# Sums of two query blocks under one guard and one reciprocal, and small VectorE operations made by GpSimd, in attention followed by a Fourier-mixing feed-forward layer

## The chip, the cores and the metric

The kernel runs on one core of one Trainium2 chip. The metric is the device time of one execution in microseconds, the median of several. The core has five engines that run side by side, each through its own list of instructions in order, and wait for one another by semaphores: PE (TensorE, matrix products), DVE (VectorE), ACT (ScalarE), POOL (GpSimd) and SP (SyncE, which here issues transfers).

## The reference

Sliding-window attention with four sink tokens (4 batches, 8 heads, 768 tokens, 64 per head, window 128), then a two-dimensional Fourier transform of the result, a layer norm and a feed-forward layer:

```python
scores = np.where(is_sink | in_window, scale * q @ k.T, -1e9)
scores = scores - np.max(scores, axis=-1, keepdims=True)
a = np.exp(scores)
a = a / (np.sum(a, axis=-1, keepdims=True) + 1e-09)
x = a @ v                                    # heads side by side: 768 x 512
u = x + np.real(np.fft.fft(np.fft.fft(x, axis=1), axis=2))
un = (u - mean(u)) / np.sqrt(var(u) + 1e-6)
out = u + np.maximum(un @ w_ch1, 0.0) @ w_ch2
```

## The kernel before

**Attention.** A batch is six blocks of 128 queries, `g` counts the 24 blocks of all batches. A block is worked in four steps, one for a pair of heads (`hp`). In each, PE makes the scores in PSUM (L701, L703), DVE merges the two key blocks (`merge`, L709) and takes mask and minimum (`soft1`, L721), ACT takes the exponential and its sum (`expo`, L727), POOL splits the sink columns (`sink_p`, L738, L739), PE transposes (L755), ACT copies (L762), POOL cuts the window by two affine_selects (`newer_p` L771, `older_p` L779), and PE multiplies with the values (`av`, L793). The tile `mx` of a block (128 x 3 x 8) holds the minima of its 8 heads in row 0, the sums in row 1, and in row 2 the guarded sums and their reciprocals: POOL adds 1e-9 (`floor`, L747), DVE inverts (`inverse`, L743), and when the block's output is in PSUM, DVE multiplies it by row 2 into `u` (`store_x`, L821).

**Order.** The program walks through 96 steps and 14 more. `STEP_LAG` and `BLOCK_AT` say how many steps behind the scores an operation stands (`floor` 6, `inverse` 8, `store_x` 13 after the first step of its block), and `SCHEDULE` the order on each engine within a step. Work of other stages hangs on steps as events, `at(step, engine, function)`, and runs at the entry "V" (DVE), "A" (ACT), "G" (POOL) or "T" (PE) of the step's list. Up to step 97 the order is as written; behind it the framework's scheduler places the instructions, and it may draw some of them forward between the written ones.

**Fourier.** When the fourth block of a batch is stored, `fourier` hangs up that batch's transform: folds of `u` (L352, L359, L362), split into a high and a low part (L365, L368), two stages of products (L395, L422, L443) and updates of `u` (L459, L460), half of the folds and, but in the last batch, most updates on POOL. The first token of a batch is worked apart. Its row `xr` is loaded in 33 copies; `put_row` (L381) copies it into `u`, `mid_sum` (L372) adds its reversed half, and `mid_row` (L376, L378) puts it, high and low, into `sph`, which the last product of the first stage reads (L395, `za<-cst_row,sph`). These four instructions hang on "V" 5, 8 and 10 steps after the folds' start.

**First group's normalisation.** `normalize` takes the statistics of the first four blocks of the first batch; `deviations` computes 1/sqrt(var) for them by a guess (L522, L524) and four Newton steps of three instructions on 128x4 (L527, L529, L531), hung on "V" of steps 72 to 80. At step 81 `un_make` (L539) normalises the first block on DVE.

**Feed-forward.** Weights are read as integers, put together on DVE (L591 to L593), split on ACT (L608) and POOL (L609); PE makes the two products (L620, L1126) for seven groups of blocks, with ACT and DVE between them (L1114, L1119). The other groups' `deviations` run on DVE. (`general` marks a second program for other parameters, which these inputs do not take.)

Of the kernel before, what the change touches and what calls it, by code (L numbers as in the profile page):

```python
# [11 lines left out]
F32 = mybir.dt.float32  # L12
# [7 lines left out]
P = 128  # L20
# [186 lines left out]
def kernel(  # L207
# [63 lines left out]
    def run(general):  # L271
        tag = "g" if general else ""
        with ExitStack() as p1:
# [59 lines left out]
            def fourier(b, at, ready):  # L333
# [35 lines left out]

                def mid_sum():  # L370
                    r = t_["x0"]
                    V.tensor_tensor(r[:, 1:256], r[:, 1:256], r[:, 511:256:-1], op=ALU.add)  # L372

                def mid_row():
                    t = t_["x0"]
                    V.tensor_copy(sph[:NR, :257], t[:, :257])  # L376
                    lo = sph[NR - 1:NR, :257]
                    V.tensor_tensor(lo, t[NR - 1:NR, :257], f32(lo), op=ALU.subtract)  # L378

                def put_row():  # L380
                    V.tensor_copy(u[NHALF][0:1], t_["x0"][0:1])  # L381
# [94 lines left out]
                at(ready[0] + ROW[0], "V", put_row)  # L476
                at(ready[0] + ROW[1], "V", mid_sum)
                at(ready[0] + ROW[2], "V", mid_row)
# [39 lines left out]
            def deviations(b, blk, n):  # L518
# [6 lines left out]
                for _ in range(4):  # L525
                    yield
                    V.scalar_tensor_tensor(t, y, -0.5, x, op0=ALU.mult, op1=ALU.mult)  # L527
                    yield
                    V.tensor_tensor(t, t, y, op=ALU.mult)  # L529
                    yield  # L530
                    V.scalar_tensor_tensor(y, t, 1.5, y, op0=ALU.add, op1=ALU.mult)  # L531
# [27 lines left out]
            def normalize(s0, s1, s2, get_bank):  # L559
# [6 lines left out]
                steps = deviations(0, 0, n)  # L566
                for i in range(14):
                    at(s1 + i * (s2 - s1) // 14, "V", lambda: next(steps, None))
# [67 lines left out]
            def window_attention(fourier, load_constants):  # L636
                with ExitStack() as pa:
# [73 lines left out]
                    def soft1(g, hp):  # L711
# [4 lines left out]
                        if hp == 0:  # L716
                            st["mx", g] = aw.tile([P, 3, H], F32, tag="mx", name=f"mx_{g}", bufs=4)
                        sm, mx = st["sm", g, hp // 2], st["mx", g]
# [5 lines left out]
                    def expo(g, hp):  # L724
                        sm, mx = st["sm", g, hp // 2], st["mx", g]
# [15 lines left out]
                    def inverse(g):  # L741
                        mx = st["mx", g]
                        V.reciprocal(mx[:, 2], mx[:, 2])  # L743

                    def floor(g):
                        mx = st["mx", g]
# [72 lines left out]
                    def store_x(g):  # L819
                        u = uview(g // NB)  # L820
                        V.tensor_tensor(u[Q_BLOCKS[g % NB]].rearrange("p (h d) -> p h d", h=H), st.pop(("x", g)),  # L821
                                        st.pop(("mx", g))[:, 2, :, None].broadcast_to([P, H, D]), op=ALU.mult)
# [516 lines left out]
```

## Time and profile before

| | before |
|---|---|
| median of 3 runs | 784.29 us (782.91 to 787.69) |
| profiled execution | 786.08 us |
| its span, first to last instruction | 784.1 us |
| busy: PE | 755.7 us (96%) |
| busy: DVE | 453.5 us (58%) |
| busy: ACT | 237.1 us (30%) |
| busy: POOL | 185.1 us (24%) |
| mean granted TensorE clock | 0.991 |

The profile is one execution. An engine is busy while one of its compute instructions runs; waiting, branching and issuing transfers do not count. Matmuls are pipelined and their ends are modelled, so a busy PE is not a PE at its peak. Attention and most of the Fourier work lie in the first 215 us, with the feed-forward layer from there to the end; the two overlap between about 180 and 300 us. Times within the span are counted from its first instruction. "<-" in a row of waits names what ended the wait.

### The profile page before, as it was taken

What the parts mean: (1) busy time and instruction counts of PE and PEld (TensorE: products, weight loads), DVE (VectorE), ACT (ScalarE), POOL (GpSimd) and SP (SyncE); (2) the same over time, 40 slices, a digit from 0 to 9 for tenths busy, and PEclk for the clock granted to TensorE, in tenths of its full rate; (3) what the DMA queues carried; (4) which work ended last, traced back from release to release, by engine and by line L of the source; (5) the groups of instructions that cost most, each with busy time, mean ns of one, the idle gap of its engine ahead of it and who ended that gap; (6) DMA issues with size and microseconds to landing.
All of it is one profiled execution on the core that took longest, in us unless ns stands there. A gap on an engine that the chain in (4) does not pass through costs nothing.

```text
span 784.1 us, 11917 instructions
## 1 busy us (share of the span) xinstructions
PE 755.7 (96%) x4379; PEld 616.8 (79%) x4379; DVE 453.5 (58%) x1330; ACT 237.1 (30%) x704; POOL 185.1 (24%) x307
## 2 busy tenths in 40 slices
PE   7999998989998999999999999999999999999996
PEld 5676876867777878899888888888888888888895
DVE  6878587999999489561456424661456424611211
ACT  4887765766523123221111101111111111110110
POOL 2567477477654255100000000000000000000000
PEclk9999999999999899999999999999999999999998
DMA  9863535434215266110100002000200001000100
GB/s 283 268 177 105 151 83 177 127 112 145 86 50 166 92 196 208 66 59 1 54 0 1 1 18 89 1 0 1 81 0 1 2 1 54 1 0 1 54 1 31
DMA packets 41810, 57.67 MB, mean 74 GB/s; under 512 B 2796, under 2 KB 27500, under 8 KB 41360
## 3 DMA queue, kind: packets, MB, share of 16 engines
q1 hardware_dynamic: 41456, 53.07, 21.6%
q0 software_dynamic: 288, 3.76, 1.3%
q8 instruction: 36, 0.59, 0.3%
q14 instruction: 30, 0.25, 0.1%
HBM read 47.37 MB, written 9.45 MB: 72 GB/s over the span
## 4 chain that ended last, share of the span: by engine, by line
PE 80%; DVE 9%; POOL 4%; issue 3%; ACT 2%; DMA 2%; SPq 1%; POOLq 0%; DVEq 0%; ACTq 0%
PE o L1126 33%; PE h L620 33%; PE s L703 3%; PE xt L793 3%; PE pt L755 2%; PE za L395 1%; DVE cv L592 1%; DVE cv L593 1%; DVE sm L721 1%; PE zb L395 1%; ACT pta L762 1%; ACT sm L727 1%; DMA vt<-in_v_sink_dram 1%; POOL ptl L771 1%; DVE s L709 1%
## 5 line engine op out<-in xcount | busy, mean ns | idle before, releaser
L1126 PE MATMUL o<-w,h 128*128 128x512 f32 x876 | 218.6, 397 | 0.0
L1119 DVE SCALAR_TENSOR_TENSOR h<-h,h 128x512 fp32r<-128x512 f32 (+1 forms) x107 | 65.4, 611 | 250.5 <-ACT h L1114 250.3
L1126 PEld LDWEIGHTS o<-w,h 128*128 128x128 f32 x876 | 164.5, 190 | 36.0
L1114 ACT ACTIVATE h<-h 128x512 fp32r<-128x512 f32 (+1 forms) x107 | 57.1, 534 | 368.6 <-PE h L620 362.4
L620 PE MATMUL h<-un_slots,w 128*128 128x512 f32 (+1 forms) x576 | 124.7, 365 | 0.0
L620 PEld LDWEIGHTS h<-un_slots,w 128*128 128x128 f32 x576 | 99.6, 188 | 19.6
L620 PE MATMUL h<-un_last,w 128*128 128x512 f32 (+1 forms) x432 | 89.0, 355 | 0.0
L620 PEld LDWEIGHTS h<-un_last,w 128*128 128x128 f32 x432 | 72.7, 188 | 12.8
L727 ACT ACTIVATE sm<-sm,mx 128x132 f32<-128x132 f32 x192 | 76.0, 400 | 6.0 <-DVE mx L721 6.0
L1150 DVE STREAM_TRANSPOSE unf<-un 32x128 f32<-32x128 f32 x224 | 67.7, 302 | 3.2
L703 PE MATMUL s<-ring,q 64*128 64x260 f32 x320 | 49.9, 418 | 8.9 <-DVE mx L721 5.3
L721 DVE CUSTOM_DVE_ANT_0 sm<-s,mask 128x132 f32<-128x132 f32 x192 | 48.5, 293 | 6.3 <-PE s L701 1.3
L703 PEld LDWEIGHTS s<-ring,q 64*128 64x128 f32 x320 | 27.3, 188 | 21.6 <-issue 8.0
L609 POOL TENSOR_TENSOR w<-cv,w 128x512 fp32r<-128x512 f32 x25 | 34.1, 1366 | 30.5 <-ACT w L608 30.5
L793 PE MATMUL xt<-ptl,ldv 128*64 128x128 f32 x384 | 39.3, 285 | 0.2 <-POOL ptl L771 0.2
L727 ACT ACTIVATION_READ_ACCUMULATOR sm<-sm,mx 128x1 f32 x192 | 36.7, 191 | 0.0
L1126 PE MATMUL o<-w_ring,h 128*128 128x512 f32 x144 | 35.6, 393 | 0.0
L762 ACT COPY pta<-pt 128x512 f32<-128x512 f32 x48 | 28.0, 583 | 24.9 <-PE pt L755 23.5
L709 DVE COPY_PREDICATED s<-older,s 128x256 f32<-128x256 uint8 x80 | 33.7, 421 | 1.6 <-PE s L703 1.6
L771 POOL TENSOR_SCALAR_AFFINE_SELECT ptl<-pta 128x512 f32<-128x512 f32 x48 | 32.5, 678 | 7.3 <-ACT pta L762 7.2
L793 PEld LDWEIGHTS xt<-ptl,ldv 128*64 128x64 f32 x384 | 21.9, 136 | 15.1 <-issue 6.2
L793 PE MATMUL xt<-pta,ldv 128*64 128x128 f32 x320 | 31.7, 274 | 0.3 <-POOL pta L779 0.3
(197 smaller groups left out, 1039.4 us busy)
## 6 DMA issues: line engine op xcount, KB each, us to landing
raw<-in_moe_w_ch_dram SPq DMA_DIRECT2D x32, 512.0 KB, 3.7
ldv<-in_v_dram SPq DMA_DIRECT2D x28, 256.0 KB, 3.3
ring<-in_qk_dram SPq DMA_DIRECT2D x24, 264.0 KB, 4.8
out_dram<-u SPq DMA_DIRECT2D x24, 256.0 KB, 2.1
q<-in_qk_dram SPq DMA_DIRECT2D x20, 256.0 KB, 4.4
cst<-in_dft_dram POOLq DMA_DIRECT2D x1, 3348.0 KB, 12.8
ud<-us SPq DMA_DIRECT2D x12, 256.0 KB, 2.1
u<-ud SPq DMA_DIRECT2D x2, 1024.0 KB, 4.9
```

The lines of the kernel that those rows point to most:

```text
L620: T.matmul(ps[:, :tb], a[:, cs], x[:, :, cc, :], start=n == 0, stop=n == 3 * NCC - 1)
L703: T.matmul(ps[:, j, :P + W], st["q", g][rows, hp, :], keys(g, 2 * hp + j), start=True, stop=True)
L709: V.copy_predicated(ps[:, :, P + NS:P + W], older[qi > 2], ps[:, :, 0:P])
L721: V.tensor_tensor_reduce(sm[:, h % 4], ps[:, j, P:P + W], mask[min(qi, 3)], -SCALE, 3.0e38, ALU.add, ALU.min, accum_out=mx[:, 0, h:h + 1])
L727: A.activation(sm[:, h % 4], sm[:, h % 4], AF.Exp, bias=mx[:, 0, h:h + 1], scale=-1.0, accum_out=mx[:, 1, h:h + 1])
L762: A.copy(a, st.pop(("pt", g, hp // 2)))
L771: G.affine_select(lo, a, [[0, 4], [s, P]], compare_op=ALU.is_ge, fill=0.0, base=0, channel_multiplier=-s)
L793: T.matmul(ps[D * j:D * j + D, p, :], st["v", kb(g) - i][:, h, :], a[:, h % 4, :], start=i == 0, stop=i == n - 1)
L1114: A.activation(h[0], ps[:, :tb], AF.Relu)
L1119: V.scalar_tensor_tensor(h[1], ps[:, :tb], 0.0, f32(h[0]), op0=ALU.max, op1=ALU.subtract)
L1126: T.matmul(po[i], a[:, ts_], x, start=f == 0 and n == 0, stop=f == NF - 1 and n == 2)
L1150: V.transpose(unf[32 * q:32 * q + 32, :, r], un[r].rearrange("p (c q j) -> p c q j", c=NCC, q=4)[:, :, q])
```

## The change

Three edits.

1. Two blocks share a tile `mx` of 128 x 3 x 2 x 8 (three buffers for four). `floor` and `inverse` do nothing for a block of even `g`, and for one of odd `g` handle both blocks, 16 columns.
2. `put_row`, `mid_sum` and `mid_row` are made by POOL, at the entry "G" of the same steps.
3. Of the first group's Newton steps all but the guess are made by POOL. A scalar_tensor_tensor becomes, in the first place, a product (the factor -0.5 goes to the third), in the third a tensor_scalar and a product: four instructions for three.

```diff
+                R = V if general else G
+
                 def mid_sum():
                     r = t_["x0"]
-                    V.tensor_tensor(r[:, 1:256], r[:, 1:256], r[:, 511:256:-1], op=ALU.add)
+                    R.tensor_tensor(r[:, 1:256], r[:, 1:256], r[:, 511:256:-1], op=ALU.add)
 
                 def mid_row():
                     t = t_["x0"]
-                    V.tensor_copy(sph[:NR, :257], t[:, :257])
+                    R.tensor_copy(sph[:NR, :257], t[:, :257])
                     lo = sph[NR - 1:NR, :257]
-                    V.tensor_tensor(lo, t[NR - 1:NR, :257], f32(lo), op=ALU.subtract)
+                    R.tensor_tensor(lo, t[NR - 1:NR, :257], f32(lo), op=ALU.subtract)
 
                 def put_row():
-                    V.tensor_copy(u[NHALF][0:1], t_["x0"][0:1])
+                    R.tensor_copy(u[NHALF][0:1], t_["x0"][0:1])
...
-                at(ready[0] + ROW[0], "V", put_row)
-                at(ready[0] + ROW[1], "V", mid_sum)
-                at(ready[0] + ROW[2], "V", mid_row)
+                at(ready[0] + ROW[0], "V" if general else "G", put_row)
+                at(ready[0] + ROW[1], "V" if general else "G", mid_sum)
+                at(ready[0] + ROW[2], "V" if general else "G", mid_row)
...
-            def deviations(b, blk, n):
+            def deviations(b, blk, n, eng=V):
...
                     yield
-                    V.scalar_tensor_tensor(t, y, -0.5, x, op0=ALU.mult, op1=ALU.mult)
+                    if eng is V:
+                        V.scalar_tensor_tensor(t, y, -0.5, x, op0=ALU.mult, op1=ALU.mult)
+                    else:
+                        G.tensor_tensor(t, y, x, op=ALU.mult)
                     yield
-                    V.tensor_tensor(t, t, y, op=ALU.mult)
+                    eng.tensor_tensor(t, t, y, op=ALU.mult)
                     yield
-                    V.scalar_tensor_tensor(y, t, 1.5, y, op0=ALU.add, op1=ALU.mult)
+                    if eng is V:
+                        V.scalar_tensor_tensor(y, t, 1.5, y, op0=ALU.add, op1=ALU.mult)
+                    else:
+                        G.tensor_scalar(t, t, -0.5, 1.5, op0=ALU.mult, op1=ALU.add)
+                        G.tensor_tensor(y, t, y, op=ALU.mult)
...
-                steps = deviations(0, 0, n)
+                steps = deviations(0, 0, n, V if general else G)
                 for i in range(14):
-                    at(s1 + i * (s2 - s1) // 14, "V", lambda: next(steps, None))
+                    at(s1 + i * (s2 - s1) // 14, "V" if i < 2 or general else "G", lambda: next(steps, None))
...
-                        if hp == 0:
-                            st["mx", g] = aw.tile([P, 3, H], F32, tag="mx", name=f"mx_{g}", bufs=4)
-                        sm, mx = st["sm", g, hp // 2], st["mx", g]
+                        if hp == 0 and g % 2 == 0:
+
+                            st["mx", g // 2] = aw.tile([P, 3, 2, H], F32, tag="mx", name=f"mx_{g}", bufs=3)
+                        sm, mx = st["sm", g, hp // 2], st["mx", g // 2][:, :, g % 2]
...
                     def inverse(g):
-                        mx = st["mx", g]
+                        if g % 2 == 0:
+                            return
+                        mx = st["mx", g // 2]
                         V.reciprocal(mx[:, 2], mx[:, 2])
 
                     def floor(g):
-                        mx = st["mx", g]
+                        if g % 2 == 0:
+                            return
+                        mx = st["mx", g // 2]
                         G.tensor_scalar_add(mx[:, 2], mx[:, 1], 1e-9)
```

What it moves, at the three places of which the prediction speaks (line numbers of the changed kernel are a few higher). First POOL at steps 76 to 78, before; `sk` are the sink columns, `ptl` and `pta` the cut probabilities, `f` a fold, `mx` the guard:

```order
L738 CAST sk_2272<-sm_0_2167 128x2x16
L739 TENSOR_TENSOR sk_2272<-sm_0_2167,sk_2272 128x2x16
L771 AFFINE_SELECT ptl_3_2300<-pta_3_2266 128x512
L352 TENSOR_TENSOR f_2_0_2302<-u_65 128x512
L779 AFFINE_SELECT pta_3_2266<-pta_3_2266 128x512
L738 CAST sk_2272<-sm_2_2240 128x2x16
L739 TENSOR_TENSOR sk_2272<-sm_2_2240,sk_2272 128x2x16
L771 AFFINE_SELECT ptl_1_2366<-pta_1_2330 128x512
L747 TENSOR_SCALAR mx_2168<-mx_2168 128x8
L359 TENSOR_TENSOR f_2_0_2293<-f_2_0_2302 128x255
```

And now; `stat` are the Newton steps, two or four rows of them in nearly every step:

```order
L748 CAST sk_2244<-sm_0_2140 128x2x16
L749 TENSOR_TENSOR sk_2244<-sm_0_2140,sk_2244 128x2x16
L532 TENSOR_TENSOR stat_0_1875<-stat_0_1875 128x4
L534 TENSOR_TENSOR stat_0_1875<-stat_0_1875 128x4
L785 AFFINE_SELECT ptl_3_2272<-pta_3_2240 128x512
L539 TENSOR_SCALAR stat_0_1875<-stat_0_1875 128x4
L540 TENSOR_TENSOR stat_0_1875<-stat_0_1875 128x4
L352 TENSOR_TENSOR f_2_0_2276<-u_65 128x512
L793 AFFINE_SELECT pta_3_2240<-pta_3_2240 128x512
L532 TENSOR_TENSOR stat_0_1875<-stat_0_1875 128x4
L534 TENSOR_TENSOR stat_0_1875<-stat_0_1875 128x4
L748 CAST sk_2244<-sm_2_2212 128x2x16
```

Between the rows of the attention there are now Newton rows, sixteen in all over nine steps; the guard of the even block is gone. The last two Newton rows stand right ahead of the next fold of this kind (`f_2_1`), a dozen rows behind this piece.

The second place is POOL in the second batch, now; `u` are updates of the first batch:

```order
L761 TENSOR_SCALAR mx_1377<-mx_1377 128x16
L359 TENSOR_TENSOR f_1_1_1645<-f_1_1_1654 128x255
L748 CAST sk_1750<-sm_0_1648 128x2x16
L749 TENSOR_TENSOR sk_1750<-sm_0_1648,sk_1750 128x2x16
L461 TENSOR_TENSOR u_64<-u_64,d_1_1641 128x257
L462 TENSOR_TENSOR u_64<-u_64,d_1_1641 128x255
L378 CAST sph<-xr_1431 33x257
L380 TENSOR_TENSOR sph<-xr_1431,sph 1x257
L785 AFFINE_SELECT ptl_3_1776<-pta_3_1744 128x512
```

The two `sph` rows stand between an update and the affine_select, where before the one followed the other; they were on DVE.

The third is POOL at the end of the attention, where the scheduler decides, before and then now:

```order
L609 TENSOR_TENSOR w_ring<-cv_3180,w_ring 128x512
L771 AFFINE_SELECT ptl_3_3074<-pta_3_3053 128x512
L779 AFFINE_SELECT pta_3_3053<-pta_3_3053 128x512
L460 TENSOR_TENSOR u_65<-u_65,d_2_3141 128x255
L459 TENSOR_TENSOR u_65<-u_65,d_2_3141 128x257
```

```order
L618 TENSOR_TENSOR w_ring<-cv_3148,w_ring 128x512
L785 AFFINE_SELECT ptl_3_3042<-pta_3_3021 128x512
L793 AFFINE_SELECT pta_3_3021<-pta_3_3021 128x512
L383 COPY us_3_2593<-xr_2996 1x512
L374 TENSOR_TENSOR xr_2996<-xr_2996 33x255
L378 CAST sph<-xr_2996 33x257
L380 TENSOR_TENSOR sph<-xr_2996,sph 1x257
L462 TENSOR_TENSOR u_65<-u_65,d_2_3109 128x255
```

All four row operations of the last batch stand in one run between the last affine_select and the first update, and are gone from DVE's list. In all, DVE has 40 instructions fewer (12 reciprocals, 12 Newton, 16 for the rows), POOL 20 more (16 Newton and 16 for the rows, less 12 guards).

## Rows read from the trace of the kernel before

**Rows 1.** The page, part 1: busy microseconds, share of the span, instructions.
```profile
PE 755.7 (96%) x4379; PEld 616.8 (79%) x4379; DVE 453.5 (58%) x1330; ACT 237.1 (30%) x704; POOL 185.1 (24%) x307
```

**Rows 2.** Busy time by stretch: length, engines' busy us, granted clock, DMA share, GB/s.
```profile
15.00:100.00 85.00, 82.36 (x747) 61.27 (x748) 64.46 (x303) 63.18 (x246) 49.42 (x109) 0.98 0.59 181
145.40:185.00 39.60, 35.77 (x319) 28.26 (x316) 38.37 (x144) 25.98 (x98) 29.58 (x50) 1.00 0.35 108
185.00:205.00 20.00, 18.42 (x163) 14.74 (x162) 17.54 (x56) 14.04 (x49) 14.29 (x26) 1.00 0.36 117
205.00:255.00 50.00, 45.75 (x266) 39.19 (x264) 49.32 (x78) 16.58 (x34) 27.46 (x22) 0.99 0.33 106
400.00:784.00 384.00, 377.38 (x1727) 310.66 (x1726) 156.44 (x407) 50.54 (x90) 0.00 (x0) 0.99 0.05 17
```

**Rows 3.** Waits of POOL, 145.4 to 185: us in total, times, longest.
```profile
POOL sk L738 <- ACT sm L727: 6.2, 5, 2.4
```

**Rows 4.** Groups on DVE, 145.4 to 185: count | busy us, mean ns | idle before.
```profile
L531 DVE SCALAR_TENSOR_TENSOR stat<-stat 128x4 f32<-128x4 f32 x4 | 2.5, 613 | 0.0
...
L529 DVE TENSOR_TENSOR stat<-stat 128x4 f32<-128x4 f32 x4 | 2.2, 546 | 0.1
...
L527 DVE SCALAR_TENSOR_TENSOR stat<-stat 128x4 f32<-128x4 f32 x4 | 1.1, 276 | 0.0
...
L743 DVE RECIPROCAL mx<-mx 128x8 f32<-128x8 f32 x4 | 0.8, 198 | 0.0
```

**Rows 5.** Groups over the whole span: operations on the first token's row.
```profile
L378 DVE TENSOR_TENSOR sph<-xr,sph 1x257 fp32r<-1x257 f32 x4 | 2.0, 498 | 0.1
...
L372 DVE TENSOR_TENSOR xr<-xr 33x255 f32<-33x255 f32 x4 | 1.6, 410 | 0.0
...
L376 DVE CAST sph<-xr 33x257 fp32r<-33x257 f32 x4 | 1.6, 398 | 0.0
...
L381 DVE COPY us<-xr 1x512 f32<-1x512 f32 x2 | 0.8, 406 | 0.0
```

**Rows 6.** Time line of DVE: start, us, line, operation, shapes.
```profile
152.43 0.19 DVE L743 RECIPROCAL mx<-mx 128x8 f32<-128x8 f32 x1
152.54 1.21 DVE L531 SCALAR_TENSOR_TENSOR stat<-stat 128x4 f32<-128x4 f32 x1
153.67 0.68 DVE L352 TENSOR_TENSOR f<-u 128x512 f32<-128x512 f32 x1
...
166.35 0.64 DVE L539 TENSOR_SCALAR un<-u,stat 128x512 f32<-128x512 f32 x1
```

**Rows 7.** Time line of POOL, the same stretch.
```profile
152.45 1.27 POOL L352 TENSOR_TENSOR f<-u 128x512 f32<-128x512 f32 x1
...
160.47 1.27 POOL L352 TENSOR_TENSOR f<-u 128x512 f32<-128x512 f32 x1
```

**Rows 8.** Groups on POOL, 145.4 to 185.
```profile
L460 POOL TENSOR_TENSOR us<-us,d 128x255 f32<-128x255 f32 x5 | 4.3, 866 | 0.0
...
L359 POOL TENSOR_TENSOR f<-f 128x255 f32<-128x255 f32 x3 | 2.3, 764 | 0.5 <-DVE f L362 0.3
...
L739 POOL TENSOR_TENSOR sk<-sm,sk 128x32 fp32r<-128x32 f32 x8 | 2.1, 268 | 0.7
...
L738 POOL CAST sk<-sm 128x32 fp32r<-128x32 f32 x8 | 1.9, 236 | 6.2 <-ACT sm L727 6.2
...
L747 POOL TENSOR_SCALAR mx<-mx 128x8 f32<-128x8 f32 x4 | 1.5, 387 | 0.3
```

**Rows 9.** Chain of work, 98 to 128: start, us, engine, tile, line.
```profile
116.65 1.05 POOL u L460
...
123.89 0.24 POOL mx L747
```

**Rows 10.** Time line of POOL: the end of the attention.
```profile
210.91 0.97 POOL L779 TENSOR_SCALAR_AFFINE_SELECT pta<-pta 128x512 f32<-128x512 f32 x1
216.31 1.85 POOL L460 TENSOR_TENSOR u<-u,d 128x255 f32<-128x255 f32 x1 [4.43 <-DVE d L448]
```

More of the change, by code (lines that the diff above doesn't have):

```diff
@@ L724, in expo @@
                     def expo(g, hp):
-                        sm, mx = st["sm", g, hp // 2], st["mx", g]
+                        sm, mx = st["sm", g, hp // 2], st["mx", g // 2][:, :, g % 2]
                         for h in range(2 * hp, 2 * hp + 2):
@@ L821, in store_x @@
                         V.tensor_tensor(u[Q_BLOCKS[g % NB]].rearrange("p (h d) -> p h d", h=H), st.pop(("x", g)),
-                                        st.pop(("mx", g))[:, 2, :, None].broadcast_to([P, H, D]), op=ALU.mult)
+                                        st["mx", g // 2][:, 2, g % 2, :, None].broadcast_to([P, H, D]), op=ALU.mult)
                     def lag(fn, s, d):
```

## The prediction

> **What bounds the kernel now.** I read the page's busy shares first: TensorE (PE) 96%, VectorE (DVE) 58%, ScalarE (ACT) 30%, GpSimd (POOL) 24% [rows 1]. They are averages over unlike stages, so the next view was busy time by stretch [rows 2]. From 400 us on PE is busy 377.4 of 384 us, POOL not at all, and nothing that the change touches runs there, so whatever the change does happens before about 260 us and shifts the rest as a block. In front of that three stretches differ. From 15 to 100 us DVE is busy 64.5 of 85 us and POOL 49.4: neither is full, and matmul time is 82.4. From 145.4 to 185 us DVE is busy 38.4 of 39.6 us: this is where all the Newton steps of the first group and the row operations of the third batch stand. POOL is busy 29.6 there, so it is idle for 10.0, and of that 6.2 are waits for ACT's exponentials [rows 3], which come from what DVE made. From 205 to 255 us DVE is busy 49.3 of 50 us, with the row operations of the last batch among the weight conversions, and POOL 27.5. So DVE sets the pace in the second and the last of these, and time taken from it there counts. PE's 35.8 of 39.6 us is weaker evidence: a busy PE here is not a PE at its peak. [...]
>
> The view that speaks against the change is the chain of work between 98 and 128 us. There the end is set by POOL: its updates of u (1.05 us the one at 116.65) through to its guard at 123.89 are one unbroken line of POOL work [rows 9], and the second batch's row operations would be put into it.
>
> **The change part by part.** *What leaves DVE from 145.4 to 185.* The twelve Newton operations on 128x4 are busy 2.5 + 2.2 + 1.1 = 5.8 us [rows 4]. That is not all their own. The one at 152.54 takes 1.21 us while POOL runs a 1.27 us tensor_tensor from 152.45, and ends when that does [rows 6, 7]. [...] The four row operations cost 0.50 + 0.41 + 0.40 + 0.41 = 1.7 us in a batch [rows 5]. Of the four reciprocals in the stretch two go, 0.4 us [rows 4]; the two that stay handle 16 columns for 8, and in 0.2 us I count nothing for that. Neighbours on DVE overlap by 0.08 us (152.43 + 0.19 against a start at 152.54 [rows 6]), for 18 instructions 1.4. DVE is relieved of 5.8 - 1.0 + 1.7 + 0.4 - 1.4 = 5.5 us.
>
> *What POOL gets there.* No POOL operation of 128x4 is in the trace. The nearest are a tensor_tensor of 128x32 at 0.27 us and a tensor_scalar of 128x8 at 0.39 [rows 8]; against that the cast of 128x32 at 0.24 bounds it from below. Sixteen operations (one scalar_tensor_tensor becomes a product, the other a tensor_scalar and a product), each waiting for the one before, at 0.29: 4.6 us, between 3.8 (16 x 0.24) and 6.2 (16 x 0.39). For the row no POOL operation with 1 or 33 partitions is shown. By the same number of columns: the sum with the reversed half is L359's form, 0.76; the subtraction of 257 columns is like L460's 255, 0.87 with its stalls, I take 0.75; the cast of 257 columns lies between 0.24 and 0.76, I take 0.4; the copy of 512, between the same, 0.6 [rows 8]. Together 2.5 us; if fewer partitions were much cheaper, down to 1.0 (four times 0.24). Two of four guards go; they are 0.39 with stalls, I count 0.3 each. POOL gets 4.6 + 2.5 - 0.6 = 6.5 us, and its work becomes 36.1 us.
>
> *So in this stretch* DVE would need 38.4 - 5.5 = 32.9 us and POOL 36.1: POOL becomes the longer one. If it is as tightly packed as DVE is now (38.4 of 39.6, 97%), the stretch takes 37.2 us, **2.4 less**. The ends: 5.5 less if only DVE counts, 6.5 more if POOL keeps all of its 10.0 idle us.
>
> *205 to 255 us.* DVE loses 1.7 - 4 x 0.08 = 1.4 us. POOL's four operations stand, in the new order, behind the affine_select at 210.91 and ahead of the update at 216.31, where POOL now sits idle for 4.43 us [rows 10], so POOL has the 2.5 us. [...] I charge half of POOL's two tensor_tensors, (0.76 + 0.75) / 2 = 0.7: **0.7 less** in sum. Ends: 1.4 less, and 1.1 more (all 2.5 us charged).
>
> [...]
>
> *98 to 128 us.* In the new order the cast and the subtraction for `sph` follow the update at 116.65, inside POOL's line, 0.4 + 0.75 and 0.1 between them; the guard at 123.89 goes, 0.3 [rows 8, 9]. **0.9 more**; between nothing (if POOL's later waits take it up) and 1.4. The copy and the sum of this batch lie ahead of a POOL wait and are hidden by it.
>
> *15 to 100 us.* The first batch's row leaves DVE and joins POOL, and neither is full (64.5 and 49.4 of 85 us) [rows 2]. Nothing; between 1.7 less and 2.5 more.
>
> *The shared guard and reciprocal.* For an even block they now come four steps later, one step ahead of its store. The guard waits for nothing else new. Where POOL is late, DVE waits at the reciprocal, and merges and score minima queue behind it; that is the same POOL lateness, counted above.
>
> *The wait of `un_make`.* DVE's normalisation at 166.35 now waits for POOL's last Newton product, which stands ahead of the fold at 160.47 [rows 6, 7]: 5.9 us of slack. POOL's extra work up to there is the 4.6, and 0.6 for the copy less 0.3 for a guard, 4.9. It holds by 1.0 us even if no idle time takes any of it up. Past that, each microsecond is a DVE stall.
>
> **Sum.** -2.4 - 0.7 + 0.9 = -2.2 us. The profiled execution took 786.08 us (span 784.1 and 2.0 around it): 783.9. It stood 1.8 us above the median of the three runs, 784.29, against which the forecast is **782.1 us**.
>
> **Rivals.**
> *A. DVE alone counts.* POOL's surplus runs over into 185 to 205 us, where it is busy 14.3 of 20 [rows 2]. Then -5.5 - 1.4 + 0.9 = -6.0: 778.3 us. For it: DVE has hardly an idle moment. Against it: 36.1 us of POOL work does not fit into 34.1 us, and the probabilities that the value products wait for would be late by the difference.
> *B. POOL becomes the bound and keeps its idle time (slower).* Its waits for ACT stay where they are and the new work is added: +6.5 - 0.7 + 0.9 = +6.7: 791.0 us. For it: the chain already runs through POOL elsewhere [rows 9], and sixteen dependent operations are spread over one line. Against it: the waits [rows 3] hang on DVE, which gets faster. It decides from the point where POOL keeps more than 39.6 - 36.1 = 3.5 of its 10.0 us.
> [...]
>
> **How the numbers follow.** Forecast (779.5 to 784.5) 0.48, A 0.20, C 0.18, B 0.14. About 1% (7.8 us) is what a measurement of this kernel can tell from no change, as its own runs lie up to 4.8 apart. Below 776.5 us lies the part of A in which the first batch's row also counts (1.7 more): 0.07. Above 792.1 lies B with the dearer price (6.2 for 4.6, so 792.6): 0.05. The rest, 0.88, is within 1%. The range leaves out 0.07 below 776.5 and the upper 0.12 (nearly all of B): 776.5 to 788.5.
>
> **What would show it.** Right: DVE's busy time falls by some 14 us in all (4.8 for the Newton steps, 4 x 1.7 for the rows, 12 x 0.2 for the reciprocals), the stretch from the first Newton step to the third batch's last row step is 1 to 4 us shorter, POOL in it above 90% busy with few waits for ACT, and everything after 300 us moved as a block. Wrong: waits of `un_make` or of the reciprocal on POOL of over 1 us (B); two-operand DVE rows that grow to over 1 us beside POOL's new ones (C); a POOL price per small operation above 0.4 us, by which the whole second stretch would be POOL's.

## The result

| | before | after |
|---|---|---|
| median of 20 runs each | 784.58 us (782.21 to 787.69) | 786.42 us (784.79 to 790.43) |
| ratio after / before | | 1.0029, 95% interval 1.0019 to 1.0040 |
| profiled execution, its span | 786.08 us, 784.1 | 786.62 us, 784.3 |

The change makes the kernel 2.3 us slower (0.0029 of 784.6). The forecast was 2.2 us faster, inside the same 1%: the sign was wrong, and the two differ by 4.5 us. Of the experiments' executions two single ones (1876 us in e11, 1229 us in e12) lie far outside all others; ratios, mean clocks and fits leave them out.

The page of after, part 1:

```profile
PE 755.4 (96%) x4379; PEld 618.0 (79%) x4379; DVE 446.0 (57%) x1290; ACT 237.0 (30%) x704; POOL 191.7 (24%) x327
```

and its busy time by stretch (columns as in [rows 2]):

```profile
15.00:100.00 85.00, 80.32 (x743) 60.29 (x743) 61.77 (x288) 62.57 (x242) 49.31 (x106) 1.00 0.58 180
145.40:185.00 39.60, 36.18 (x328) 28.63 (x325) 34.55 (x127) 26.46 (x100) 34.86 (x69) 1.00 0.36 107
...
205.00:255.00 50.00, 45.96 (x253) 40.26 (x253) 47.55 (x71) 15.71 (x32) 27.37 (x26) 0.93 0.31 97
```

From 145.4 to 185 us VectorE is relieved (38.4 to 34.6 us) and GpSimd takes it (29.6 to 34.9), as meant; yet the score minima at 184 us start within 0.1 us of where they did: what had been lost ahead of 147 us, 0.8, was gained behind it, and no more. In all, VectorE's busy time fell by 7.5 us, not by 14, in part because the rows that stayed on it became longer (4.4 us in sum). From 205 to 255 us the granted clock is 0.93, for 0.99 in [rows 2]; before has its fall from 254 to 261 us, with 0.50 from 255 to 260.

**Two sources of time, kept apart.** The spans of executions of one kernel go with their mean granted clock. Over all kernels of this study, with one level for each kernel and one slope, 0.001 of mean clock goes with 0.44 us of span. The kernel before has a mean clock of 0.9956 (162 executions), after 0.9927 (20). So 2.9 x 0.44 = 1.3 us of the loss goes with TensorE's clock, and at equal clock after is 1.2 us longer (0.8 to 1.6). The second part is that of the list of instructions, and can be placed.

**Where it is placed.** In the two profiles I took the start of the same instruction (score minima up to 192 us, then feed-forward matmuls) and subtracted. The table gives what each stretch added to the lateness against the profile of before, in us. The last stretch is to be read with care: there the profile of before itself lost (0.08 + 0.50 + 0.10) x 5 = 3.4 us of clock, so that a kernel which loses none there (the first row alone) stands at -2.8 without any merit. Elsewhere in the table clock was lost in two fields, marked *.

| kernel | 58 to 81 | 98 to 137 | 147 to 192 | 192 to 217 | 217 to 283 | clock lost there |
|---|---|---|---|---|---|---|
| after | +1.0 | +0.5* | -0.7 | +1.1 | -0.9 | 3.4 |
| all four rows on GpSimd | +0.8 | +1.1 | -0.6 | +1.1 | -2.3 | 1.7 |
| Newton steps on GpSimd | 0.0 | 0.0 | -0.3 | 0.0 | -1.1 | 1.7 |
| Newton steps left out | 0.0 | 0.0 | -0.3 | 0.0 | -1.4 | 1.7 |
| guards shared | +0.1 | -0.6 | -0.3 | 0.0 | -1.3 | 1.7 |
| reciprocals shared | 0.0 | 0.0 | -0.2 | 0.0 | -1.6 | 1.7 |
| first row on GpSimd | +0.9 | 0.0 | 0.0 | 0.0 | -2.8 | 0 |
| second row on GpSimd | 0.0 | +1.1 | 0.0 | 0.0 | -1.4 | 1.7 |
| last row on GpSimd | 0.0 | 0.0 | 0.0 | +1.1 | -2.5 | 1.7 |
| after, cast and subtraction on VectorE | +0.3 | -0.6 | -0.6 | +0.9 | -2.7 | 1.7 |
| cast and subtraction alone on GpSimd | +0.4 | +1.2 | +0.2 | +0.7* | -3.4 | 0 |

In the table each stretch has the same value in every kernel that has the same edit, to about 0.3 us, although the kernels ran on different chips. (The whole change with the last row left on VectorE has +0.7 from 98 to 137 us with no clock lost there, which suggests that the loss in the marked field of after lay beside other waits.) Three kernels outside the table have 1.9 to 2.7 us from 98 to 137 us: the pairing alone and the pairing with copies on ScalarE (e1, e11), which lost 1.7 of clock there, and three rows on GpSimd (e4), in which TensorE waits 2.8 us for a transfer of values. From 147 to 192 us the edits do not add up: the third row alone has -0.6, pairing and Newton steps without it (e16) -0.6 as well, all together -0.7. A difference of medians is less sharp: a dozen executions hold different clock losses.

Lateness arises at three places. **First, the first batch's row, near 66 us.** GpSimd's time line of after (start, us):

```profile
64.20 0.25 POOL L749 TENSOR_TENSOR sk<-sm,sk 128x32 fp32r<-128x32 f32 x1
64.40 0.39 POOL L378 CAST sph<-xr 33x257 fp32r<-33x257 f32 x1
64.87 0.72 POOL L380 TENSOR_TENSOR sph<-xr,sph 1x257 fp32r<-1x257 f32 x1
65.67 0.64 POOL L785 TENSOR_SCALAR_AFFINE_SELECT ptl<-pta 128x512 f32<-128x512 f32 x1
66.27 1.43 POOL L352 TENSOR_TENSOR f<-u 128x512 f32<-128x512 f32 x1
67.66 0.63 POOL L793 TENSOR_SCALAR_AFFINE_SELECT pta<-pta 128x512 f32<-128x512 f32 x1
```

and what TensorE waits for from 62 to 76 us in after (in all, times, longest):

```profile
PE xt L807 <- POOL pta L793: 1.4, 1, 1.4
```

The two affine_selects in before:

```profile
65.29 0.63 POOL L771 TENSOR_SCALAR_AFFINE_SELECT ptl<-pta 128x512 f32<-128x512 f32 x1
67.12 0.82 POOL L779 TENSOR_SCALAR_AFFINE_SELECT pta<-pta 128x512 f32<-128x512 f32 x1
```

Cast and subtraction take 64.40 to 65.6 us, in a row without an idle moment. After, which was 0.9 us ahead of before at 58 us, starts the selects behind them 0.4 and 0.5 us later than before, and the value product waits 1.4 us for the second. In the profile of before no wait of TensorE on GpSimd stands in this stretch.

**Second, the second batch's row, near 118 us**, the same picture on GpSimd's time line of after:

```profile
116.29 1.08 POOL L462 TENSOR_TENSOR u<-u,d 128x255 f32<-128x255 f32 x1
117.33 0.85 POOL L378 CAST sph<-xr 33x257 fp32r<-33x257 f32 x1
118.26 0.72 POOL L380 TENSOR_TENSOR sph<-xr,sph 1x257 fp32r<-1x257 f32 x1
119.05 0.64 POOL L785 TENSOR_SCALAR_AFFINE_SELECT ptl<-pta 128x512 f32<-128x512 f32 x1
```

and TensorE's wait from 108 to 130 us:

```profile
PE xt L807 <- POOL pta L793: 1.0, 1, 1.0
```

**Third, the last batch's row, near 213 us.** GpSimd's time line of after:

```profile
211.99 0.79 POOL L383 COPY us<-xr 1x512 f32<-1x512 f32 x1
212.87 0.78 POOL L374 TENSOR_TENSOR xr<-xr 33x255 f32<-33x255 f32 x1
213.72 0.47 POOL L378 CAST sph<-xr 33x257 fp32r<-33x257 f32 x1
214.27 1.05 POOL L380 TENSOR_TENSOR sph<-xr,sph 1x257 fp32r<-1x257 f32 x1
```

and VectorE's beside it:

```profile
212.24 0.83 DVE L600 TENSOR_SCALAR cv<-raw 128x512 int32<-128x512 int32 x1
212.99 0.94 DVE L359 TENSOR_TENSOR f<-f 128x255 f32<-128x255 f32 x1
213.85 0.88 DVE L601 SCALAR_TENSOR_TENSOR cv<-raw,cv 128x512 int32<-128x512 int32 x1
214.66 0.68 DVE L835 TENSOR_TENSOR us<-x,mx 128x512 f32<-128x512 f32 x1
```

In before, where GpSimd is idle at this time [rows 10], VectorE's fold, conversion and store read

```profile
212.42 0.40 DVE L359 TENSOR_TENSOR f<-f 128x255 f32<-128x255 f32 x1
213.08 0.41 DVE L591 TENSOR_SCALAR cv<-raw 128x512 int32<-128x512 int32 x1
213.42 0.67 DVE L821 TENSOR_TENSOR us<-x,mx 128x512 f32<-128x512 f32 x1
```

and the second part of the conversion (L601 in after) takes 0.67 us in the kernel with the copies on ScalarE, below. The store at 214.66 is 1.2 us later than in before, after a lateness of 0.2 at the store ahead of it. The trace shows the lengths, not their cause: beside GpSimd's run of four rows the fold takes 0.94 for 0.40 us, the conversion 0.83 for 0.41 and its second part 0.88 for 0.67, while the store at 214.66, still beside GpSimd's subtraction, takes 0.68 for 0.67. Of GpSimd's rows the cast takes 0.47 and the subtraction 1.05 us here, for 0.39 and 0.72 near 66 us. An expectation below calls VectorE's lengthening the shut-out. By 283 us most of it is given back: TensorE's wait of 2.6 us near 253 us is not there in after, which has its own of 2.6 near 228. Both profiles lost 3.4 us of clock there, so +1.1 and -0.9 can be added: in this pair of profiles the place is worth about 0.2 us. The run with the last row alone, below, has 0.6 (0.2 to 1.1) at equal clock.

**And the gain that did not come.** The chain of work in after, 157 to 164 us:

```profile
157.61 1.02 PE xt L807 x16
158.64 0.55 PE a L424 x3
...
159.72 0.58 ACT pta L776
160.30 0.29 ACT asb L433
...
160.63 1.00 PE b L445 x6
...
161.73 0.42 DVE d L450
...
163.52 1.14 DVE f L352
```

then, in after, VectorE's longest wait from 145.4 to 185 us, and GpSimd's for ScalarE:

```profile
DVE d L450 <- PE b L445: 2.5, 1, 2.5
```

```profile
POOL sk L748 <- ACT sm L737: 1.2, 3, 0.6
```

At 154.7 us VectorE is 2.2 us further ahead than at 146.5; at 165 us it has lost 1.4 of that, as it stands 2.5 us before the product `b`, which TensorE makes in its own order at 160.63. The profiles of before and after list no wait of TensorE from 145 us up to this product, and there it waits for two copies of ScalarE, `pta` and `asb`. In before this wait is as long:

```profile
PE b L443 <- ACT asb L431: 1.0, 1, 1.0
```

So the wait that VectorE's lead runs into hangs on the lists of TensorE and ScalarE. Some of VectorE's rows become longer as well, and not only where GpSimd has new ones: the split L368 takes 1.12 us at 162.40 for 0.68 in before, and 1.11 in the sixth kernel below, where GpSimd got nothing. Behind the third batch's row VectorE's fold L352 at 172.98 takes 1.75 us, for 1.12 in before, beside a fold of GpSimd's own of 1.71 us at 172.48, for 1.43 in before. GpSimd's waits for ScalarE fell from 6.2 us [rows 3] to 1.2, one of 1.4 for VectorE's guess came, and no row of VectorE waits for the Newton steps.

### The profile page after: what moved, and what is told of

It reads as the page before. It is cut to its first block, busy times and chain, and to the rows that moved or that the text cites. A ratio compares the mean times of both kernels' runs of the same rounds, so it can differ in the third digit from the quotient of the medians.

```text
span 784.3 us, 11897 instructions
## 1 busy us (share of the span) xinstructions
PE 755.4 (96%) x4379; PEld 618.0 (79%) x4379; DVE 446.0 (57%) x1290; ACT 237.0 (30%) x704; POOL 191.7 (24%) x327
## 4 chain that ended last, share of the span: by engine, by line
PE 79%; DVE 10%; POOL 4%; ACT 2%; issue 2%; DMA 1%; SPq 0%; DVEq 0%; ACTq 0%; POOLq 0%
PE o L1140 33%; PE h L629 32%; PE xt L807 4%; PE s L712 3%; PE za L397 2%; PE pt L769 2%; DVE cv L601 1%; DVE cv L600 1%; DVE cv L602 1%; ACT pta L776 1%; PE zb L397 1%; DVE f L352 1%; DVE sm L731 1%; POOL ptl L785 1%; ACT sm L737 1%
## 5 line engine op out<-in xcount | busy, mean ns | idle before, releaser
L1140 PEld LDWEIGHTS o<-w,h 128*128 128x128 f32 x876 | 162.8, 188 | 35.5
```

The source lines that it names most:

```text
L1140: T.matmul(po[i], a[:, ts_], x, start=f == 0 and n == 0, stop=f == NF - 1 and n == 2)
```

## The experiments

All against the kernel before, run beside them on the same chip; medians of 11 to 13 executions.

| run | median us | before | ratio, 95% interval | mean clock |
|---|---|---|---|---|
| e1_mx | 781.92 | 784.01 | 0.9975 (0.9960 to 0.9990) | 0.9975 |
| e2_rows | 787.12 | 784.01 | 1.0041 (1.0028 to 1.0053) | 0.9929 |
| e3_newton | 784.26 | 784.01 | 0.9998 (0.9980 to 1.0016) | 0.9957 |
| e4_rows012 | 785.18 | 784.01 | 1.0016 (1.0002 to 1.0030) | 0.9953 |
| e5_all_but_last_row | 785.01 | 784.29 | 1.0014 (0.9993 to 1.0035) | 0.9952 |
| e6_no_newton | 783.62 | 784.29 | 0.9996 (0.9984 to 1.0008) | 0.9959 |
| e7_no_last_row | 783.37 | 784.29 | 0.9989 (0.9975 to 1.0002) | 0.9962 |
| e8_no_rows012 | 782.75 | 784.29 | 0.9984 (0.9970 to 0.9999) | 0.9946 |
| e9_recip_pair | 783.93 | 784.69 | 0.9997 (0.9979 to 1.0014) | 0.9956 |
| e10_guard_pair | 783.67 | 784.69 | 0.9986 (0.9970 to 1.0002) | 0.9968 |
| e11_mx_act | 780.84 | 784.69 | 0.9955 (0.9940 to 0.9971) | 0.9970 |
| e12_last_row_only | 784.88 | 784.69 | 0.9999 (0.9979 to 1.0018) | 0.9960 |
| e13_row0 | 785.71 | 783.90 | 1.0024 (1.0009 to 1.0039) | 0.9954 |
| e14_row1 | 785.54 | 783.90 | 1.0027 (1.0014 to 1.0040) | 0.9941 |
| e15_after_mid_row_V | 783.08 | 783.90 | 0.9983 (0.9968 to 0.9998) | 0.9963 |
| e16_after_last_only | 784.02 | 783.90 | 1.0007 (0.9994 to 1.0019) | 0.9945 |
| e17_mid_row_only | 785.22 | 784.50 | 1.0002 (0.9985 to 1.0018) | 0.9950 |
| e18_mx_act012 | 782.99 | 784.50 | 0.9976 (0.9958 to 0.9994) | 0.9958 |

### One part of the change at a time

The theory drawn from the two profiles: the row operations lose, above all in the last batch; the Newton steps are worth nothing; the pairing is small. The rival: the Newton steps on GpSimd are the loss.

The first kernel has edit 1 of the change's diff alone, the second edit 2, the third edit 3. The fourth has edit 2 with this for its choice of engine:

```diff
-                R = V if general else G
+                R = G if (not general and b < B - 1) else V
```

> Only the shared guard and reciprocal; rows and Newton steps stay on DVE. If the loss of 1.8 us lies in the last batch's row on POOL (theory T, the tail), this is within 0.5 us of before, or up to 1 us faster, since 12 reciprocals of 0.2 us leave DVE and 12 guards leave POOL. If the pairing itself costs (an even block's reciprocal comes one step ahead of its store, theory M), it is 1 us or more slower, and waits at the reciprocal grow.

> Only the row operations on POOL, in all four batches. T expects the whole loss here: 1.5 to 2.5 us slower than before, with DVE's folds and conversions from 212 to 216 us stretched to 0.8 us and more beside POOL's four row operations. The theory that POOL's load between 145 and 185 us costs the time (theory B) expects 0.5 us or less here.

> Only the first group's Newton steps on POOL; nothing else in any engine's order changes. T expects no difference (within 0.5 us): the 4 us that DVE gains are not used, because PE stands without a gap from 145 to 160 us and DVE then waits for it. B expects 1 to 2 us slower, as 16 operations join POOL where it has 10 us of idle time. Rival A of the prediction expects 3 to 4 us faster.

> The row operations on POOL in the first three batches, the last batch's on DVE as before. T expects within 0.5 us of before, and by the difference to the run with all four batches the tail's price, about 2 us. B expects this slower by 0.5 to 1 us, in the second batch's stretch from 98 to 128 us, where the chain runs through POOL (the prediction's +0.9).

Measured: pairing -2.0 us, rows +3.2, Newton steps 0, three rows +1.2. So the rows lose and the Newton steps are worth nothing; the pairing gained where nearly nothing had been forecast. Part of that is clock: at equal clock the pairing gains 0.7 us (0.2 to 1.1), the rows cost 1.6, the Newton steps 0.0 and three rows 1.0 (each ± 0.5). That theory had the three rows within 0.5 us: there it was wrong, the last batch is not the only place.

### Is the time of VectorE worth anything where it was thought to set the pace?

The fifth kernel is the whole change with the choice of engine of the fourth. In the sixth, the seventh and the eighth work is left out, not moved:

```diff
-                for i in range(14):
+                for i in range(14 if general else 2):
```

```diff
-                at(ready[0] + ROW[0], "V", put_row)
+                if general or not (b == B - 1):
+                    at(ready[0] + ROW[0], "V", put_row)
...
```

(and so for `mid_sum` and `mid_row`; in the eighth `b < B - 1`).

> The whole change, but with the last batch's row operations left on VectorE. If the parts add up (pairing -2.1, rows of the first three batches +1.2, Newton steps 0, each from its own run): about 0.9 us less than before, ratio 0.9985 to 1.0000, and so some 3 us less than the whole change. If the loss of the change lies in the sum of GpSimd's load over the attention and not in the last batch's place, it stays slower than before by 1 to 2 us.

> Before, with the first group's Newton steps left out (only the guess is kept, so that group is normalised with a rough 1/sqrt(var)); GpSimd gets nothing for it. The prediction's term (VectorE at 97% sets the pace from 145 to 185 us, 4.8 us of its work counts): 3.5 to 5 us less than before. The theory that TensorE's list, which has no gap from 145 to 160 us, takes the freed time: at most 1 us less. If it is 2 us or more, the time was there and GpSimd's sixteen operations took it back.

> Before, with the last batch's row operations left out (its first token's row is not transformed; the product reads the row of the batch before). VectorE is relieved of 1.7 us, GpSimd gets nothing. If VectorE sets the pace in the tail, as the prediction has it: 1.4 us less than before. If the pace is set elsewhere there: no change within 0.5 us, and the 2 us that the last batch's row costs on GpSimd are all the price of GpSimd's operations and of the place they get.

> Before, with the row operations of the first three batches left out (their first tokens' rows are not transformed). VectorE is relieved of 3 x 1.7 = 5.1 us, GpSimd gets nothing. The prediction: about 1.4 us less for the third batch, nothing for the first two, so 1 to 2 us less. [...]

The sixth decides the largest term of the forecast. Its busy time from 145.4 to 185 us, and VectorE's longest wait there:

```profile
145.40:185.00 39.60, 36.08 (x319) 28.46 (x319) 35.57 (x134) 25.98 (x98) 30.05 (x53) 1.00 0.36 109
```

```profile
DVE d L448 <- PE b L443: 2.1, 1, 2.1
```

With the Newton steps gone and nothing given to GpSimd, the stretch gains 0.3 us, the same as with the steps on GpSimd, and the wait for the product is there again. The product starts at 160.12 us in before and at 159.35 in the sixth kernel, which is 0.7 us ahead at 146.5 us already: it comes no earlier. So the time was not taken back by GpSimd: in this order of TensorE and ScalarE it was not there to be had. Leaving out the rows of three batches gains 1.3 us; by stretches 0.7 (58 to 81), 0.3 (98 to 137) and 0.6 (147 to 192), and in the last of these moving the row to GpSimd gives the same 0.6. Leaving out the last row gives 0.9 us, with an interval that reaches to nothing; from 192 to 217 us it gives 0.1. The fifth kernel misses: the three parts, each alone, add to -0.9, measured +1.1 (-0.5 to +2.7). By stretches it has +1.0, +0.7 and -0.6 where after has +1.0, +0.5 and -0.7, and nothing from 192 to 217 us. A part of the miss is that the gains from 147 to 192 us do not add up.

### Which half of the pairing, and two other places for the row

The ninth kernel gives each block its guard again, the tenth its reciprocal; the eleventh has the pairing and the row's copies on ScalarE; the twelfth has edit 2 for the last batch alone.

```diff
                     def floor(g):
-                        if g % 2 == 0:
-                            return
-                        mx = st["mx", g // 2]
+                        mx = st["mx", g // 2][:, :, g % 2]
                         G.tensor_scalar_add(mx[:, 2], mx[:, 1], 1e-9)
```

```diff
-                        V.reciprocal(mx[:, 2], mx[:, 2])
+                        for e in range(2):
+                            V.reciprocal(mx[:, 2, e], mx[:, 2, e])
```

```diff
+                def mid_hi():
+                    A.copy(sph[:NR, :257], t_["x0"][:, :257])
+
                 def put_row():
-                    V.tensor_copy(u[NHALF][0:1], t_["x0"][0:1])
+                    A.copy(u[NHALF][0:1], t_["x0"][0:1])
...
-                at(ready[0] + ROW[0], "V", put_row)
+                at(ready[0] + ROW[0], "A", put_row)
                 at(ready[0] + ROW[1], "V", mid_sum)
+                at(ready[0] + ROW[1] + 1, "A", mid_hi)
```

> The shared tile with only the reciprocal made for two blocks at once; the guards stay one for each block at their own times. GpSimd does what it did before, VectorE has 12 reciprocals of 0.2 us fewer. If the 2 us that the full pairing gained come from VectorE: about 782 us, ratio 0.9965 to 0.999, with most executions at a mean granted clock of 0.998 or more, as with the full pairing. If they come from GpSimd's 12 guards of 0.39 us: no change within 0.7 us.

> The shared tile with only the guard made for two blocks at once; each block keeps a reciprocal of its own, both made at the odd block's time. GpSimd has 12 guards of 0.39 us fewer, VectorE as many instructions as before. If the gain of the pairing comes from GpSimd: about 782 us and a mean granted clock of 0.997 or more. If it comes from VectorE's list: no change within 0.7 us.

> The full pairing, and of the row operations the two copies (into u, and the high part into sph) on ScalarE in all batches; the sum and the subtraction stay on VectorE. ScalarE is busy 30% and no fold or conversion of VectorE waits for it. If VectorE's relief from the rows is worth what leaving three of them out showed (1.3 us for four operations each), half of that adds to the pairing: 780.5 to 781.5 us. If the order that ScalarE's copies take in its list delays the exponentials or the copies that the products wait for, it stands at the pairing's 782 us or above.

> Before, with only the last batch's row operations on GpSimd. By the difference of the runs with four and with three rows moved: 1.5 to 2 us more than before. If the loss is TensorE's clock, which falls behind a wait of about 2.5 us near 228 us, the mean granted clock of its executions is near 0.993, and none reaches 0.998; at equal clock it would be within 0.7 us of before. If it is the shut-out of VectorE by GpSimd's rows, it is 1 us or more above before at equal clock too. If the four together make the loss and the last alone does not, no change.

Neither half alone has the pairing's 2 us: -0.2 and -1.1 us by the ratios, both intervals with no change in them, and at equal clock -0.2 and 0.0 (± 0.5). By stretches the guard's half is seen: 0.6 us from 98 to 137 (every kernel with the shared tile loses about 0.25 again from 137 to 147), where the guard at 123.89 us [rows 9] is gone from GpSimd's line. In the tenth kernel, the select and the fold that stood around it:

```profile
122.71 0.63 POOL L784 TENSOR_SCALAR_AFFINE_SELECT pta<-pta 128x512 f32<-128x512 f32 x1
123.31 0.72 POOL L359 TENSOR_TENSOR f<-f 128x255 f32<-128x255 f32 x1
```

The last row alone costs nothing by the ratio, 0.6 us (0.2 to 1.1) at equal clock; of the three cases in its expectation the one of the clock falls (mean 0.9960, one execution at 0.998 or more), the one of the shut-out asked for 1 us or more, which lies near the upper end of the 0.6, and the third (only beside the others) is what the medians say. The eleventh kernel is the fastest of all, 3.5 us under before and 5.8 under the whole change by the ratios, and 2.5 (2.0 to 3.0) under before at equal clock. TensorE's longest wait behind 212 us, 2.6 us in before, is in it

```profile
PE a L424 <- DVE zb L412: 1.1, 1, 1.1
```

### Which row, which operations

The thirteenth and the fourteenth have edit 2 with `b == 0` and `b == 1`. The fifteenth is the whole change but for

```diff
-                    R.tensor_copy(sph[:NR, :257], t[:, :257])
+                    V.tensor_copy(sph[:NR, :257], t[:, :257])
...
-                    R.tensor_tensor(lo, t[NR - 1:NR, :257], f32(lo), op=ALU.subtract)
+                    V.tensor_tensor(lo, t[NR - 1:NR, :257], f32(lo), op=ALU.subtract)
```

with `mid_row` on "V" again; the seventeenth is before with these two lines alone on GpSimd. The sixteenth is the whole change with edit 2 for `b == B - 1` alone. The eighteenth is the eleventh with the last batch's copies on VectorE.

> Before, with only the first batch's row operations on GpSimd. The profile of the run with three rows moved shows the cast and the subtraction (0.39 and 0.72 us) ahead of an affine_select in a stretch near 66 us where GpSimd has no idle time, and TensorE waiting 1.4 us for the next one. If that holds, 1.0 us more than before, and the steps behind 72 us are all later by that. The prediction had nothing for this batch: no change within 0.4 us.

> Before, with only the second batch's row operations on GpSimd. The prediction: 0.9 us more, for the cast and the subtraction in GpSimd's unbroken line near 117 us. If the three rows' 1.1 us at equal clock are all the first batch's, no change within 0.4 us, because GpSimd's later waits for ScalarE take it up.

> The whole change, with only the cast and the subtraction of the row (all batches) left on VectorE; the copy into u and the sum stay on GpSimd. If the loss of the first batches comes from these two in GpSimd's line, about 1 us of the whole change's loss goes, more if the last batch's lies in the same two: 784.5 to 785.5 us, and 1 us or more below the whole change. If the loss comes from the sheer load of GpSimd or from the copy and the sum, it stays within 0.5 us of the whole change (786.4).

> The whole change, with the row operations of the first three batches left on VectorE; the last batch's stay on GpSimd. If terms add up by the runs so far at equal clock (first three rows 1.1, last 0.6): 785.3 us, 1.1 us below the whole change, and the granted clock 0.996 as with the last row alone. If the low granted clock of the whole change (mean 0.9927) comes with the last row in its place beside the pairing or the Newton steps, the clock stays at 0.993, none of its executions reaches 0.998, and the time is 786 us.

> Before, with only the cast and the subtraction of the row on GpSimd, in all four batches. If these two in GpSimd's unbroken lines are the loss of the change, this alone has all of it and more, as nothing makes up for it: 786 to 788 us, ratio 1.0025 to 1.005, as with all four row operations (1.0041). If the copy and the sum have a part in the loss, it is at least 1 us below that.

> The full pairing, and the row's two copies on ScalarE in the first three batches only; the last batch's stay on VectorE. If the 1.1 us that this gained over the pairing alone comes from the last batch, where TensorE's wait near 257 us fell from 2.6 to 1.1 us: back to the pairing's 782 us. If it comes from the first three batches: 781 us.

The first row alone costs 1.9 us (0.7 to 3.1), the second 2.1 (1.1 to 3.1); at equal clock 1.3 and 0.8 (± 0.5). TensorE's waits in the one from 62 to 76 us, then in the other from 108 to 132 us:

```profile
PE xt L795 <- POOL pta L781: 1.4, 1, 1.4
```

```profile
PE xt L795 <- POOL pta L781: 1.1, 2, 1.0
```

The fifteenth kernel decides: with the cast and the subtraction back on VectorE, and all else of the change kept, the kernel is 1.3 us faster than before (0.2 to 2.5), 3.6 faster than the whole change by the ratios and 1.9 at equal clock. The waits of TensorE on GpSimd near 66 and 119 us are gone from its trace. With the rows of the first three batches back the change (the sixteenth kernel) is level with before (+0.5, -0.5 to +1.5); three of its executions reach a clock of 0.998, which speaks against the second case of its expectation.

The seventeenth missed. The two operations alone cost 0.2 us (-1.2 to +1.4) where 2 to 4 were expected, and 0.6 (0.1 to 1.1) at equal clock; its time line has the +1.2 of the second batch, only 0.4 for the first, and the waits of TensorE in both places (0.7 and 1.0 us). So the copy and the sum have a part in the first batch (0.3 to 0.5 us, as the fifteenth kernel has from its side), and behind 217 us more comes back than in the others; why, the runs do not show. The eighteenth stands at -1.9 us (-3.3 to -0.5), within its interval the pairing's. At equal clock it has -0.9 and the eleventh -2.5 (± 0.5): the copies on ScalarE gain in the last batch.

## Why the prediction was wrong

**The term of -2.4 us (145 to 185) failed**, at the sentence that set TensorE's 35.8 of 39.6 us aside as weaker evidence. VectorE was busy 97%, but its rows stand between products that TensorE makes in its own order, and TensorE's list had no listed wait from 145 us up to the one for ScalarE's copies near 159 us, which is 1.0 us long with the Newton steps and without them. What VectorE saved became a wait of 2.5 us for the product behind them. Shown by leaving the work out: 0.3 us. The third row alone gives 0.6, and with it, the pairing and the Newton steps together the stretch gained no more than 0.7. The prices were not at fault: GpSimd's Newton operations took

```profile
L534 POOL TENSOR_TENSOR stat<-stat 128x4 f32<-128x4 f32 x4 | 0.8, 202 | 0.3
...
L539 POOL TENSOR_SCALAR stat<-stat 128x4 f32<-128x4 f32 x4 | 0.8, 198 | 0.1
```

0.20 us each (0.28 from start to start, 147.43 to 147.71) for 0.29 estimated, and the four of the third row 0.60 + 0.72 + 0.39 + 0.73 = 2.4 us for 2.5; those of the last row, beside VectorE's, 3.1. GpSimd came to 34.9 us for 36.1.

**Two terms of the sum are shown by no run.** The 1.0 us taken back for the fold behind the Newton operation at 152.54: in after that fold (L352 at 152.37) takes 0.63 us, for 0.68 in before. And the 0.7 us charged from 205 to 255 us as half of GpSimd's two tensor_tensors: beside the four rows VectorE's own became longer by 0.42 + 0.54 + 0.21 = 1.2 us.

**15 to 100 us, counted as nothing, measured +1.0.** The step was read from averages (64.5 and 49.4 of 85 us). GpSimd's line was read for 98 to 128 us, but not here, and near 66 us there is the same unbroken line. The upper end that the forecast gave, 2.5, held it.

**98 to 128 us, +0.9, was right** in place and mechanism: the row alone +1.1, the shared guard -0.6, the two together +0.5.

**205 to 255 us, -0.7.** The row operations fit into GpSimd's idle time, as said, and VectorE's rows beside them became 1.2 us longer: +1.1 at 217 us, the term's upper end. VectorE's relief of 1.4 us was worth nothing up to there: leaving the row out gains 0.1. That most of it comes back by 283 us was not foreseen; together about +0.2.

**The shared guard and reciprocal**, counted at 0.3 us for a guard and 0.4 inside the first term: 0.7 us at equal clock, 2.0 by the medians.

**The wait of `un_make`** was right: VectorE does not wait for the Newton steps.

**The clock** has no term in the sum. It is half of the measured loss: 1.3 us goes with a lower mean clock. This is the sum by stretches: +1.0 + 0.5 - 0.7 + 0.2 + about 0.2 (137 to 147 us) = +1.2, which is what the fit gives at equal clock. Term by term against the forecast: -2.2 + 1.7 (145 to 185) + 1.0 (15 to 100) - 0.4 (98 to 128) + 0.9 (205 to 255) + 0.2 = +1.2, and 1.3 of clock. The time lies within the range because the range reached up to 788.5 us, not by the forecast's mechanism.

**The rivals.** C, the case in which VectorE loses as much time as GpSimd gets (-5.5 + 6.5 + 1.1 + 0.9 = +3.0, so 787.3 us), came nearest in time, but not by its sum: VectorE's rows beside GpSimd's became longer in the last batch, by 1.2 us, and the fold behind the third row by 0.63 (1.75 for 1.12), but the stretch from 145 to 185 us, where C has +1.0, became 0.7 shorter, and leaving the third row out gains the same 0.6 as moving it. A row of over 1 us was to be its sign; such rows stand in before as well (1.12). A falls with the sixth run. B falls, as the stretch did not become longer although GpSimd kept 4.7 of its 10.0 idle us, more than the 3.5 from which B was to decide; its waits for ScalarE went from 6.2 to 1.2 us.

What stays open: why the mean granted clock is near 0.993 only where all four rows are moved whole (0.9927 and 0.9929; with the last row alone 0.9960 and 0.9945, without it 0.9952 and 0.9953). The traces show falls behind waits of TensorE, but not which wait is followed by one: in after the fall near 122 us stands right behind the second row's wait of 1.0 us, and the fourteenth kernel has the same wait and no fall there. Not measured either: what the 2.5 us of VectorE's wait would give if TensorE made the product `b`, and ScalarE its copy, earlier in their lists.

## What to carry over

A share of 97% does not say that an engine sets the pace: here TensorE, which it feeds, had no wait for it in the first 15 us that its relief could have closed. Before counting relief, look for the product or copy that the relieved engine will stand before, or leave the work out once and see what the stretch gains. When work is put on an engine with idle time on the average, read its line at the very place: 1.1 us of work in a line without a gap, ahead of what TensorE waits for, cost 1.0 us where GpSimd was busy 58% on the average (15 to 100 us) and 1.1 where it was busy 81% (100 to 128). Small differences of two profiles are read by stretches, with the granted clock of each beside them.

## What was not expected of the hardware

In three rows of after GpSimd took the same time for about as many columns on 1, on 33 and on 128 partitions: 0.72 us for the subtraction of 1x257 at 64.87, for the sum of 33x255 at 165.12 and for the fold of 128x255 at 114.43.

The granted clock differs between executions of one kernel, and with it the time: of before one took 789.26 us at a mean clock of 0.987, another 782.00 at 0.999. Busy time by stretch, first before, then after, then the pairing alone:

```profile
250.00:255.00 5.00, 2.38 (x15) 1.94 (x13) 4.75 (x6) 1.66 (x4) 2.40 (x2) 0.92 0.59 205
255.00:260.00 5.00, 5.00 (x16) 4.26 (x17) 0.69 (x1) 1.08 (x3) 1.28 (x1) 0.50 0.32 105
260.00:265.00 5.00, 5.00 (x25) 4.26 (x24) 0.03 (x1) 0.60 (x1) 0.00 (x0) 0.90 0.01 3
```

```profile
225.00:230.00 5.00, 2.41 (x13) 2.21 (x12) 5.00 (x12) 1.90 (x4) 0.91 (x1) 0.79 0.26 72
230.00:235.00 5.00, 5.00 (x18) 5.00 (x18) 3.45 (x7) 0.48 (x1) 1.69 (x3) 0.53 0.14 41
```

```profile
255.00:260.00 5.00, 2.49 (x18) 2.17 (x17) 4.25 (x7) 2.45 (x6) 2.42 (x2) 1.00 0.53 169
```

In the first two TensorE is busy for only 2.4 of 5 us, in a wait of 2.6 us, and then has a mean clock of 0.50 and 0.53 over 5 us. In the third it is busy for 2.49 of 5, and the clock stays at 1.00. Of the executions of before, 51 of 162 had a mean of 0.998 or more; of after, none of 20.
